# A new order of the same steps in a fused attention and token-mixing kernel

## The chip, the cores and the metric

The kernel runs on one core of one Trainium2 chip. The metric is the device time of one execution in microseconds (us); the kernel before took 115.36 us as the median of 13 runs, from 114.9 to 115.99. Five engines work side by side: PE (TensorE, matmuls and transposes), ACT (ScalarE), DVE (VectorE), POOL (GpSimd) and SP (SyncE). Each runs its own program in order, and they wait for one another and for DMA transfers through semaphores.

## The reference

There are eight batches of eight heads, 576 positions and a head size of 64. First, 32 packed queries `p` per head attend to `k` and `v`; the result is at once key and value of a second attention, with `q` as its queries. The heads are then laid side by side into `x` (576 x 512), which goes through a mixing of tokens with a ReLU and a last product.

```python
p_packed = sm_attn(p, k, v)
x = heads_side_by_side(sm_attn(q, p_packed, p_packed))
wq, wk = x @ w_q, x @ w_k
W_tok = scale * einsum('bsd,btd->bst', wq, wk)
out = maximum(einsum('bst,btd->bsd', W_tok, x), 0) @ w_out
```

## The kernel before

One batch is one round of the same chain of steps, and the rounds of neighbouring batches overlap. The name of a step is its kind, its batch and its part: `S1.3.2` is part 2 of step S1 of batch 3. In the order in which one batch needs them:

- KT transposes k (PE, L298; for batch 0 from float32), and KE copies the result out of PSUM. S1 multiplies it with the packed queries (PE, L322), X1 is the exponential on ACT (L328), and PV multiplies with v (PE, L340). RC and PP (L345, L349) divide and mask on DVE, PT transposes (L356), and PE (the step) copies.
- The packed queries of all batches are prepared once by PX (L257, L268) and PXE.
- QT transposes q (PE, L386), QE copies. S2 multiplies with the packed result (PE, L405), X2 is the exponential on ACT (L414), RS and RR sum and invert on DVE (L421, L425), and AM multiplies the two (L431) on POOL or on DVE. AT transposes that (PE, L440), AE copies.
- QK multiplies the packed result with the weights of the mixture (PE, L365), QKE copies; WC, once, copies a part of these weights on POOL (L133). WKQ forms both projections (PE, L456 and L461), WE and WR copy them, GM and Y reduce over tokens (PE, L478 and L488) with GE and YE as copies, MX and MR mix (PE, L504 and L509), and RL and RLR apply the ReLU.
- OT multiplies with w_out (PE, L536), OE copies to SBUF, and the stores go out on the queue of SP (the very last on that of ACT).

WARM steps (L603) are matmuls on zeros, without use for the output; there are ten of them, of 256 to 1024 columns in float32.

The loads are LD steps. `LD.K0` and `LD.K1` (the halves of k of batch 0), `LD.p0` and `LD.p1` go over the queues of ACT and SP. All others are issued by POOL: `P` (the packed queries of the other batches), `q`, `k` and `v` of a batch (576 KB each), `W` (four transfers for both weights of the mixture) and `O` (two transfers for w_out). k and q have four buffers each, so have the v tiles. POOL issues these loads in its own program, between its AM and WC steps; the wait of a load for its buffer or its place is thus a wait of POOL.

All of this is put into one sequence by the string ORDER (L10 on), written out in full. Every word is a step, with the PSUM bank after `=` and the engine after `@` (A for ACT, V for DVE, P for POOL). The loop at the end walks through it and emits the instructions in that order, so the order of the words is the order of each engine's program:

```python
for item in ORDER.split():
    name, _, bk = item.partition("=")
    name, _, eng = name.partition("@")
    f = name.split(".")
    if f[0] == "LD":
        d = load(f[1])
        if item == end:
            release(d)
```

`end` is the last LD of the string. Stores that come before it in the order are held, and start only when that load has landed; those after it go out as they come.

The softmax here doesn't subtract the row's maximum and nothing guards it: scores larger than these inputs give would overflow.

## Time and profile before

| | |
|---|---|
| median of 13 runs | 115.36 us |
| the profiled execution | 115.01 us |
| its span, first to last instruction | 113.0 us |
| granted TensorE clock | 0.997 |
| PE busy | 104.2 us |
| ACT, DVE, POOL busy | 82.9, 73.3, 38.3 us |
| DMA, mean | 225 GB/s |
| loads of POOL's queue, share of 16 engines | 73.6% |

The span is the time from the first to the last instruction of the profiled execution; 2.0 us lie around it. PE here is the busy time of matmuls; PEld, where it stands, is that of weight loads, which overlap matmuls. The idle time of an instruction's engine just before it stands in square brackets, with the event that ended it; that event is inferred from semaphores, and the last one is named where several were waited for. A landing is the time from the issue of a DMA to its last byte.

### The profile page before, as it was taken

Reading aid. Unit: us, or ns where it says so; the run is one execution under the profiler, and the core shown is the slowest. Engines: PE = TensorE matmul, PEld = TensorE weight load, DVE = VectorE, ACT = ScalarE, POOL = GpSimd, SP = SyncE. Lnnn points to the kernel's source line nnn. Section 1 sums busy time; section 2 is a strip of 40 time slices with the busy share of each in tenths; the row PEclk is TensorE's granted clock in tenths of the full one; section 3 lists DMA queues with packets and bytes.
Section 4 is the critical chain, followed back from the end, with each engine's and each line's share of the span. In section 5 each row is a group of like instructions: output and inputs, shape, how many; then the busy total and the mean of one; then the engine's idle time right before and its main releaser. Section 6 shows DMA issues by size and latency. Waiting matters only on the chain.

```text
span 113.0 us, 4280 instructions
## 1 busy us (share of the span) xinstructions
PE 104.2 (92%) x1842; PEld 73.5 (65%) x1855; DVE 73.3 (65%) x186; ACT 82.9 (73%) x169; POOL 38.3 (34%) x49
## 2 busy tenths in 40 slices
PE   4899979999999999999999999999999999999910
PEld 2167967588785867698858786794985664644500
DVE  2053767966897567797785898389688484916300
ACT  0008595998995896799988866997999989958420
POOL 6952226692290000558093094013008053000000
PEclk9999999999999999999999999999999999999998
DMA  1999999999999999999999999991899999993994
GB/s 50 377 219 204 208 192 208 211 203 208 206 210 211 209 213 207 215 203 208 210 208 208 217 206 201 202 191 35 286 295 321 304 355 315 321 319 100 299 315 133
DMA packets 16035, 25.44 MB, mean 225 GB/s; under 512 B 2656, under 2 KB 10848, under 8 KB 16016
## 3 DMA queue, kind: packets, MB, share of 16 engines
q0 software_dynamic: 11792, 14.42, 73.6%
q1 hardware_dynamic: 3872, 9.90, 26.5%
q10 hardware_dynamic: 352, 0.85, 2.2%
q8 instruction: 14, 0.23, 0.7%
q14 instruction: 5, 0.04, 0.1%
HBM read 30.15 MB, written 9.44 MB: 350 GB/s over the span
## 4 chain that ended last, share of the span: by engine, by line
PE 84%; ACT 6%; DMA 4%; issue 1%
PE out_ps L536 28%; PE kT_ps L298 8%; PE qT_ps L386 7%; PE pv_ps L340 6%; PE aT_ps L440 5%; DMA k_sb<-in_k_dram 4%; PE e_ps L322 4%; PE wkq_ps L461 4%; PE e_ps L405 4%; PE mix_ps L504 4%; PE warm_ps L603 4%; PE wkq_ps L456 2%; PE g_ps L478 2%; PE y_ps L488 2%; PE pqk_ps L365 1%; PE px_ps L268 1%
## 5 line engine op out<-in xcount | busy, mean ns | idle before, releaser
L431 POOL TENSOR_TENSOR a<-e,rr 128x512 bf16<-128x512 f32 (+1 forms) x13 | 16.1, 1245 | 45.8 <-DVE rr L425 22.2
L536 PE MATMUL out_ps<-wout,relu 128*128 128x512 bf16 (+1 forms) x120 | 30.6, 373 | 0.6
L131 ACT ACTIVATE o<-out_ps 128x512 f32<-128x512 f32 (+1 forms) x26 | 15.3, 590 | 7.6 <-PE out_ps L536 7.4
L536 PEld LDWEIGHTS <-relu 128*128 128x128 bf16 x132 | 11.7, 98 | 10.1 <-issue 0.3
L421 DVE TENSOR_REDUCE rs<-e 128x16 f32<-128x512 f32 (+1 forms) x16 | 12.9, 809 | 3.2 <-ACT e L414 3.0
L514 ACT ACTIVATE relu<-mix_ps 128x512 bf16<-128x512 f32 x21 | 11.5, 607 | 1.4 <-PE pv_ps L340 1.2
L603 PE MATMUL warm_ps<-warm 128*128 128x512 f32 (+1 forms) x24 | 10.8, 580 | 1.5 <-DVE warm L138 1.5
L414 ACT ACTIVATE e<-e_ps 128x512 f32<-128x512 f32 (+1 forms) x24 | 11.6, 529 | 0.7 <-PE e_ps L405 0.5
L131 ACT ACTIVATE qT<-qT_ps 128x1024 bf16<-128x1024 bf16 (+1 forms) x12 | 9.8, 831 | 2.4 <-PE qT_ps L386 2.4
L328 ACT ACTIVATE e<-e_ps 128x512 bf16<-128x512 f32 (+1 forms) x24 | 11.2, 501 | 0.2 <-PE e_ps L322 0.2
L386 PE MATMUL qT_ps<-idb,q_sb 128*64 128x128 bf16 x288 | 10.9, 220 | 0.0
L298 PE MATMUL kT_ps<-idb,k_sb 128*128 128x128 bf16 x126 | 9.9, 220 | 0.0
L386 PEld LDWEIGHTS <-q_sb 128*64 128x64 bf16 x288 | 8.8, 110 | 0.7 <-issue 0.3
L135 DVE COPY kT<-kT_ps 128x1024 bf16<-128x1024 bf16 (+1 forms) x14 | 7.8, 565 | 2.0 <-PE kT_ps L298 2.0
L516 DVE TENSOR_SCALAR relu<-mix_ps 128x512 bf16<-128x512 f32 x11 | 7.3, 686 | 2.6 <-PE mix_ps L504 2.0
L340 PE MATMUL pv_ps<-v_sb,e 64*64 64x192 bf16 x288 | 8.4, 244 | 0.6 <-ACT e L328 0.6
L298 PEld LDWEIGHTS <-k_sb 128*128 128x128 bf16 x126 | 7.5, 98 | 1.3 <-issue 0.4
L461 PE MATMUL wkq_ps<-aT,pqk 128*128 128x256 bf16 (+1 forms) x64 | 7.9, 233 | 0.0
L131 ACT ACT_TABLE_LOAD x1 | 1.3, 1283 | 8.7 <-DVE idb L210 8.7
L135 DVE COPY o<-out_ps 128x512 f32<-128x512 f32 (+1 forms) x7 | 4.6, 653 | 4.7 <-PE out_ps L536 3.7
L182 POOL DMA_DIRECT2D k_sb<-in_k_dram x7 | 5.3, 763 | 6.3 <-PE warm_ps L603 2.7
L322 PE MATMUL e_ps<-pdiag,kT 128*64 128x64 bf16 x288 | 7.4, 197 | 0.0
(81 smaller groups left out, 199.6 us busy)
## 6 DMA issues: line engine op xcount, KB each, us to landing
out_dram<-o SPq DMA_DIRECT2D x31, 256.0 KB, 3.9
q_sb<-in_q_dram POOLq DMA_DIRECT2D x8, 576.0 KB, 13.1
v_sb<-in_v_dram POOLq DMA_DIRECT2D x8, 576.0 KB, 11.7
k_sb<-in_k_dram POOLq DMA_DIRECT2D x7, 576.0 KB, 13.2
out_dram<-o_rem SPq DMA_DIRECT2D x4, 256.0 KB, 3.8
k_sb<-in_k_dram ACTq DMA_DIRECT2D x1, 576.0 KB, 4.9
k_sb<-in_k_dram SPq DMA_DIRECT2D x1, 576.0 KB, 7.5
wout<-in_moe_w_out_dram POOLq DMA_DIRECT2D x2, 256.0 KB, 12.5
```

What stands on the lines that cost most here:

```text
L131: nc.scalar.activation(o, i, COPY)
L135: nc.vector.tensor_copy(o, i)
L298: nc.tensor.transpose(ps[:, n], src[:, o:o + P], idb if b else idf)
L322: nc.tensor.matmul(ps[halves(i), at[0]:at[1] + 1:at[1] - at[0]], T["kT", b][:, place(b, m), halves(i)], rhs, start=True, stop=True)
L340: nc.tensor.matmul(T["pv", b][i][halves(cc)], lhsT, rhs, start=n == 0, stop=n == R - 1, skip_group_check=True)
L386: nc.tensor.transpose(o[halves(x)], q_in[b][:, x, r * Dh:(r + 1) * Dh], idb)
L414: nc.scalar.activation(e2(b, min(c, 1))[:, o:o + n], T["s2", b, c].rearrange("a t i c (x l) -> a (t i c x) l", l=L), EXP, scale=scale)
L421: e.tensor_reduce(rs, T["e2", (b, d)], axis=AX, op=ADD)
L431: e.tensor_tensor(a2[:, 2 * d:2 * d + n].rearrange("a t i (u l) -> a (t i u) l", l=L), T["e2", (b, d)], T["rr", (b, d)].to_broadcast((P, n ...
L461: nc.tensor.matmul(ps[:, e:e + c1 - c0], pqk[:, i, Dl:], aT[:, i, c0:c1], start=i == 0, stop=i == 1)
L536: nc.tensor.matmul(ps, lhsT, wout[:, j, x:x + w], start=j == 0, stop=j == NJ - 1)
L603: nc.tensor.matmul(ps[:, 0:n], warm[:, 0:P], warm[:, 0:n], start=True, stop=True)
```

## The change

The string ORDER is replaced by another. It has the same 664 steps, with the same shapes; their sequence differs nearly throughout, 90 of them are given to another engine for the copy or the elementwise operation, and most have another PSUM bank. Nothing else in the file changes. The order in which POOL issues its loads:

```
before: P q0 v0 k1 W q1 v1 k2 k3 O v2 q2 v3 q3 k4 q4 k5 v4 q5 k6 v5 q6 q7 k7 v6 v7
after:  P q0 v0 W k1 q1 v1 k2 k3 O v2 q2 v3 k4 q3 k5 v4 q4 k6 q5 v5 q6 v6 k7 v7 q7
```

The beginning and the end of both strings (the first 16 and the last few lines of each):

```diff
-LD.p0 LD.K0 LD.K1 LD.p1 LD.P SET.warm@V LD.q0 SET.aT1@V WARM.0=0 SET.idf@V LD.v0 SET.aff@P
-KT.0.0=1 KT.0.1=2 WARM.1=3 PX.0=4 LD.k1 KT.0.3=5 KT.0.4=6 KE.0.0@V KE.0.1@V LD.W SET.pd0@V
-PXE.0.1@A SET.idb@V PXE.0.0@A KE.0.4@V KE.0.3@V KT.0.2=7 PX.1=0 PX.2=1 LD.q1 QT.0.1=2 KE.0.2@A
-SET.v0@V S1.0.1=3 QE.0.1@A QT.0.0=4 S1.0.0=6 S1.0.2=5 PX.8=7 SET.mask@V X1.0.1@A X1.0.2@A X1.0.0@A
-PV.0.0=2,3 QT.0.2=5 SET.pd1@V LD.v1 QE.0.0@A LD.k2 PXE.8.1@V RC.0.1@V RC.0.0@V SET.v1@V WARM.5=6
-WARM.6=4 PXE.2.1@A SET.aT0@V LD.k3 WARM.9=6 PP.0.0@V PP.0.1@V QE.0.2@V PT.0=4 PE.0@A KT.1.2=2
-WARM.2=3 S2.0.0=5 KT.1.1=6 PXE.1.0@V LD.O S2.0.1=4 PXE.2.0@A S2.0.2=3 KT.1.0=1 SET.v2@V X2.0.0@A
-RS.0.0@V RR.0.0@V X2.0.2@A X2.0.1@A KE.1.0@A AM.0.0@P RS.0.1@V WARM.7=5 WC.0@P RR.0.1@V WARM.8=3
-WARM.4=5 PXE.8.0@A AT.0.0=4 KE.1.1@V KE.1.2@A S1.1.0=3 LD.v2 S1.1.2=1 QT.1.0=5 PXE.1.1@A AE.0.0@A
-QT.1.1=7 SET.wm@V SET.aT2@V AM.0.1@V X1.1.0@A QK.0=2 QKE.0@A S1.1.1=6 X1.1.1@A QT.1.2=0 AT.0.1=4
-WKQ.0.0=3 AT.0.2=2 X1.1.2@A PV.1.0=6,1 QE.1.0@V AE.0.1@A PV.1.1 AE.0.2@V PV.1.2 WE.0.0@A QE.1.1@A
-RC.1.0@V WKQ.0.2=5 WKQ.0.1=2 WARM.3=4 RC.1.1@V WE.0.1@A PP.1.0@V LD.q2 QE.1.2@A LD.v3 PP.1.1@V
-PT.1=3 WR.0@V GM.0=7 PE.1@V S2.1.0=6 GE.0@V S2.1.1=1 KT.2.2=4 Y.0=5 KT.2.0=2 LD.q3 KE.2.2@V
-S2.1.2=0 X2.1.0@A RS.1.0@V YE.0@A X2.1.1@A MX.0.0=3,7 MX.0.1=6,4 KE.2.0@V X2.1.2@A KT.2.1=5 LD.k4
-RL.0.0@A S1.2.0=1 RR.1.0@V QK.1=0 S1.2.2=2 KT.3.2=3 RL.0.3@A AM.1.0@P KT.3.1=4 RL.0.2@A RS.1.1@V
-QKE.1@A X1.2.2@A AT.1.0=7 KE.3.2@A KT.3.0=0 RL.0.1@A RR.1.1@V AM.1.1@V AT.1.2=2 AE.1.0@V AE.1.2@A
...
-RL.6.2@V RL.6.3@A RL.6.1@V WKQ.7.0=3 RL.6.0@A WE.7.0@A OE.5.4@V WKQ.7.1=1 WKQ.7.2=4 MR.6=0
-WE.7.1@V RLR.6@A OT.6.2=6 WR.7@V OE.6.2@A GM.7=5 GE.7@A OT.6.1=7 Y.7=2 OT.6.3=3 YE.7@V OE.6.1@A
-MX.7.0=1,0 MX.7.1=4,6 MR.7=5 RL.7.2@V OE.6.3@A RLR.7@A OT.6.0=7 RL.7.0@V OT.7.4=2 RL.7.1@A
-RL.7.3@A OT.7.2=3 OT.7.3=0 OE.6.0@V OE.7.4@A OT.7.1.1=5 OE.7.3@A OE.7.2@V OT.7.1.0=1 OE.7.1.0@A
-OT.7.0=4 OE.7.1.1@V OE.7.0@A
+LD.p0 LD.K0 LD.K1 LD.p1 SET.warm@V SET.aT1@V SET.mask@V SET.pd0@V LD.P LD.q0 WARM.1=0 LD.v0
+SET.idf@V SET.aff@P PX.0=1 KT.0.0=2 SET.v1@V LD.W WARM.0=3 SET.wm@V KT.0.3=4 KT.0.2=5 SET.idb@V
+SET.pd1@V KE.0.0@A KT.0.1=6 KT.0.4=7 WARM.3=0 PX.1=2 KE.0.1@A LD.k1 QT.0.2=3 QT.0.0=0 KE.0.3@A
+PXE.0.0@V KE.0.2@V PXE.0.1@A SET.aT0@V LD.q1 SET.v0@V KE.0.4@V S1.0.2=5 S1.0.0=6 LD.v1 X1.0.0@A
+QT.0.1=4 S1.0.1=7 X1.0.1@A X1.0.2@A QE.0.0@V QE.0.2@A WARM.9=1 PV.0.0=0,6 RC.0.0@V LD.k2 WARM.8=7
+PX.2=5 QE.0.1@A PP.0.0@V LD.k3 RC.0.1@V PXE.1.1@A LD.O PP.0.1@V PT.0=1 PX.8=3 PE.0@V SET.aT2@V
+PXE.2.0@A S2.0.0=4 S2.0.2=0 X2.0.0@A WARM.6=7 PXE.8.1@A S2.0.1=6 SET.v2@V WC.0@P WARM.7=1
+PXE.8.0@V KT.1.2=7 KT.1.0=4 RS.0.0@V LD.v2 KE.1.2@V X2.0.1@A X2.0.2@A RR.0.0@V RS.0.1@V LD.q2
+KT.1.1=3 S1.1.2=1 QK.0=6 LD.v3 WARM.2=7 KE.1.1@V RR.0.1@V AM.0.0@P AT.0.0=0 LD.k4 AM.0.1@V
+PXE.1.0@A KE.1.0@A S1.1.1=2 X1.1.2@A QT.1.1=7 S1.1.0=4 AE.0.0@V PXE.2.1@A QT.1.2=3 X1.1.1@A
+QKE.0@A LD.q3 AT.0.1=1 AT.0.2=5 QE.1.2@V X1.1.0@A AE.0.2@V WKQ.0.0=2 WKQ.0.2=0 WARM.4=6 WE.0.0@A
+AE.0.1@V WKQ.0.1=3 WR.0@V WE.0.1@V PV.1.0=5,4 PV.1.1 PV.1.2 RC.1.0@V RC.1.1@V QT.1.0=1 GM.0=6
+PP.1.0@V PP.1.1@V PT.1=2 WARM.5=0 QE.1.1@A QE.1.0@V GE.0@A PE.1@A Y.0=7 S2.1.2=3 S2.1.0=5 X2.1.0@A
+KT.2.2=4 S2.1.1=6 YE.0@V X2.1.1@A MR.0=1 KT.2.0=0 KE.2.2@V RS.1.0@V S1.2.2=2 X2.1.2@A QK.1=7
+MX.0.1=4,5 RR.1.0@V RLR.0@A X1.2.2@A QKE.1@A MX.0.0=6,3 AM.1.0@P RS.1.1@V RL.0.0@A KT.2.1=1
+KT.3.2=2 KE.2.0@A RR.1.1@V AM.1.1@P KE.3.2@V KE.2.1@V KT.3.0=7 KT.3.1=6 AT.1.0=2 AE.1.0@V S1.2.1=1
...
+AT.7.0=2 OE.5.0@A AM.7.1@V RLR.4@V QKE.7@A AT.7.2=7 YE.6@V MR.5=0 AT.7.1=6 AE.7.1@A AE.7.2@V
+MX.6.1=4,1 AE.7.0@A RLR.5@V MX.6.0=3,5 RL.6.1@V RL.6.0@A OT.5.4=7 RL.6.3@V WKQ.7.2=0 WKQ.7.1=6
+OE.5.4@V RL.6.2@A WE.7.1@A WKQ.7.0=4 WR.7@V WE.7.0@A OT.6.3=2 GM.7=3 OT.6.2=1 MR.6=5 OE.6.3@A
+GE.7@A Y.7=7 OT.6.1=0 YE.7@V RLR.6@V MX.7.0=6,4 MX.7.1=2,3 MR.7=7 RL.7.0@V OE.6.2@A OT.6.0=1
+OE.6.1@A RL.7.3@A RLR.7@V OT.7.4=5 RL.7.2@V RL.7.1@A OT.7.2=0 OE.6.0@A OT.7.3=6 OT.7.1.1=3
+OT.7.1.0=7 OE.7.1.1@V OE.7.4@A OT.7.0=2 OE.7.2@A OE.7.3@A OE.7.1.0@V OE.7.0@A
```

In POOL's program the first AM step, `AM.0.0@P`, and the copy `WC.0@P` stand after the loads of O and before v2 in the order before; in the order after, WC stands there, and AM.0.0 stands after v3.

## The prediction

> **What bounds the kernel now.** I read the shares of busy time first, then what PE waited for, then PE, POOL and the landings in order of time. PE carries the page:

> ```profile
> PE 104.2 (92%) x1842; PEld 73.5 (65%) x1855; DVE 73.3 (65%) x186; ACT 82.9 (73%) x169; POOL 38.3 (34%) x49
> ```

> The waits of PE (line waited for: us in all, times, longest) are three, all before 15 us:

> ```profile
> PE warm_ps L603 <- DVE warm L138: 1.5, 1, 1.5
> PE pv_ps L340 <- ACT e L328: 0.6, 1, 0.6
> PE kT_ps L298 <- DMA k_sb<-in_k_dram: 0.5, 1, 0.5
> ```

> Busy time by stretches (PE first, then PEld, DVE, ACT, POOL) says that from 22.1 us to the last matmul at 107.7 PE is full:

> ```profile
> 0.00:22.10 22.10, 19.42 (x239) 13.07 (x239) 11.65 (x34) 10.71 (x18) 11.18 (x21) 1.00 1.07 208
> 22.10:76.80 54.70, 54.24 (x1196) 41.88 (x1204) 41.63 (x105) 46.57 (x100) 21.69 (x25) 1.00 1.17 207
> 76.80:107.70 30.90, 30.54 (x410) 18.54 (x414) 19.97 (x49) 25.02 (x53) 5.46 (x5) 1.00 0.82 271
> ```

> So the end is the moment at which PE's dense run starts, plus a fixed amount of matmul work, plus any bubble that a new order puts into it, plus 5.3 us of last eviction and store. The dense run starts with AT.0.0 (aT_ps, L440), which transposes the output of AM.0.0 on POOL (a, L431). PE in order of time (start, us) around it:

> ```profile
> 20.05 1.94 PE L603 MATMUL warm_ps<-warm 128*128 128x256 f32 x6
> 22.13 0.40 PE L440 MATMUL aT_ps<-idb,a 128*128 128x128 bf16 x4
> ```

> And POOL, which issues the loads and runs AM.0.0 in one program:

> ```profile
> 9.14 0.71 POOL L186 DMA_DIRECT2D q_sb<-in_q_dram  x1 [2.07 <-DMA pbf<-in_p_dram]
> 12.05 0.76 POOL L178 DMA_DIRECT2D v_sb<-in_v_dram  x1 [2.20 <-DMA q_sb<-in_q_dram]
> 14.65 0.74 POOL L182 DMA_DIRECT2D k_sb<-in_k_dram  x1 [1.84 <-DMA v_sb<-in_v_dram]
> 18.06 0.74 POOL L182 DMA_DIRECT2D k_sb<-in_k_dram  x1 [2.67 <-PE warm_ps L603]
> 18.79 1.24 POOL L174 DMA_DIRECT2D wout<-in_moe_w_out_dram  x2
> 21.03 1.05 POOL L431 TENSOR_TENSOR a<-e,rr 128x512 bf16<-128x512 f32 x1 [1.00 <-DVE rr L425]
> 22.03 0.39 POOL L133 COPY wqk<-wqk 128x256 bf16<-128x256 bf16 x1
> 22.37 0.81 POOL L178 DMA_DIRECT2D v_sb<-in_v_dram  x1
> 23.17 0.72 POOL L186 DMA_DIRECT2D q_sb<-in_q_dram  x1
> 23.87 0.79 POOL L178 DMA_DIRECT2D v_sb<-in_v_dram  x1
> ```

> Count POOL's DMAs: P, q0, v0, k1, four of W, then q1 is the ninth, and it waits until the first (P) has landed; v1, the tenth, waits for the second (q0); k2 for the third. Issue plus time to landing: P 1.27+7.6 = 8.9, q1 issued 9.14; q0 1.98+9.8 = 11.8, v1 issued 12.05; k1 3.83+13.7 = 17.5, k3 (twelfth, four after eight) issued 18.06; k2 (eleventh) 14.65+11.9 = 26.5, k4 (nineteenth) issued 27.11. The names on the last two idle times are other engines, but the landings fit. So each DMA of POOL waits for the landing of the one eight places earlier, and is issued 0.25 to 0.55 us after it.

> [...] POOL idles 2.07 us before q1. [...] POOL here runs in program order throughout. [...]

> **The change, part by part.** *Work.* The 664 steps are the same set, so PE's work is the same: 275 PE steps, with equal sums. Ninety steps change engine. Priced by the rows of each form (AE 0.611 on ACT, 0.415 on DVE; RLR 0.466, 0.423; WE 0.502, 0.552; YE 0.386, 0.425; QKE 0.506, 0.550; AM of 128x768 1.480 on POOL, 0.940 on DVE), ACT loses 3.3 us, DVE gains 3.3, POOL loses 1.9. They stay near 71%, 68% and 32%, so I cost this at nothing: PE hides it. Without that cover DVE's 3.3 us would be the price.

> *Front, up to AT.0.0 on PE.* The first warm matmuls end at 5.24 as now. Then PX.0, KT.0.0 and WARM.0 (about 0.8, 0.6 and 1.8) fill until 8.5; K1 lands at 1.19+7.5 = 8.7; four groups KT.0.* (0.5, 0.5, 0.5, 0.2), WARM.3 (0.5) and PX.1 (0.5) reach 11.4; q0 lands at 11.8; QT.0, S1.0 and WARM.9 (0.14+0.5+0.06+0.27+0.5+0.27+0.86) reach 14.6; v0 is there at 2.74+11.6 = 14.3. PV.0 (0.9) ends at 15.5, against 15.84 now. Then, up to AT.0.0: WARM.8 0.86, PX.2 0.75, PT.0 0.13, PX.8 0.74, S2.0.0 and S2.0.2 0.5, WARM.6 0.5, S2.0.1 0.25, WARM.7 0.5, KT.1 1.0, S1.1.2 0.16, QK.0 0.27, WARM.2 0.5: 6.2, so PE is at AT.0.0 at 21.7. Set on its own chain, AM.0.0 could start at 20.5: X2.0.0 ends at 18.8, RS.0.0 0.69, then KE.1.2 (0.28, after KT.1.2 at 19.9) stands before RR.0.0 (0.25). It would be done by 21.6 and PE would not wait.

> *POOL.* But AM.0.0 is moved. Now it stands right behind the two loads of O. In the new program POOL has q1, v1, k2, k3, O, O, WC.0, v2, q2, v3, and only then AM.0.0. v2 (0.81) and q2 (0.72) have free places (W has long landed; q2 waits for k1, at about 18.2, W now being ahead of it). v3 is the seventeenth DMA and waits for the ninth, q1. The bytes ahead of q1 are the same set in both orders and the DMA engines are full (share 1.07), so it lands as now:

> ```profile
> q_sb<-in_q_dram POOLq DMA_DIRECT2D x1, 576.0 KB, 11.8
> ```

> that is 9.14+11.8 = 20.9. v3 is issued 0.25 to 0.55 later and takes 0.79: 22.0 to 22.3. AM.0.0 takes 1.05: 23.05 to 23.35. AT.0.0 follows 0.05 later, as now, at 23.1 to 23.4, after a PE stall of about 1.5 us; behind it in PE's order stand S1.1.1, QT.1.1 and all the rest.

> *Sum.* AT.0.0 moves from 22.13 to 23.1..23.4: +1.0 to +1.3. The steps of PE left from there are longer by QK.0's, S1.1.2's and WARM.3's absence against WARM.4 and WARM.5: sums 82.74 against 82.48, times 1.04 for changes of operation: +0.27. Together +1.25 to +1.55; I take +1.35, the earlier issue being what three of the five waits show. The next chain is covered: QKE.0 on ACT, behind S1.1.1 and X1.1.1, ends at about 24.7, and WKQ.0.0, which needs it, is reached at 25.2.

> *Later loads.* k4 moves ahead of q3, k5 and v4 ahead of q4, k6 of q5, v6 of k7, q7 to the end. Landings come every 2.85 us or so and the places are shared out anew. By PE's summed steps the new order needs q2 at about 39.8 (lands 37.7), k5 at 51.5 (49.6), q4 at 56.6 (54.8); the others have more. Now the smallest margins are k7's (lands 59.55+13.2 = 72.75, used at 72.77) and q4's (49.6, used at 50.31). So nothing is lost, and nothing large was there to win. The other AMs behind loads (AM.1.0 behind q3, which waits for k2 at 26.5 and is out by 27.8; AM.2.1 behind k6, 34.9; AM.3.0 behind q5, 37.7) are wanted 3 us and more later. The last load ends at about 77 as now, so the held stores start as now. The last seven OT stand in the same order and the last eviction is on ACT again (0.60): nothing.

> The profiled execution took 115.01 us, 113.0 of span and 2.0 around it. Its sum is 113.0+1.35+2.0 = 116.4. The median of the runs, 115.36, is 0.35 above that execution, so the forecast is 116.7.

> **Rivals.** (1) *Not slower: POOL isn't held.* If v3 gets its place before about 19.7, AM.0.0 starts at 20.5 and AT.0.0 is reached at 21.7 to 21.8: -0.35, plus 0.27, about -0.1, hence 115.3. It decides if q1 lands by 19.5 rather than 20.9, or if v3's wait is for an older DMA. For it: v3 in the trace of before was issued long after q1 landed, so its own wait isn't seen. Against: five other loads show the rule of eight. If ACT's front also runs shorter than my 0.9 us a copy, and the earlier PP.0 (two memsets, 0.54 and 0.12, no longer stand before it) is worth its 0.7 us, it would be 114.6.
> (2) *More bubbles.* Short covers in the new order are GM.2 to Y.2 (0.35 us of PE work for an eviction of 0.28 and its hand-over), AT.0.2 to WKQ.0.2 (0.37 for 0.22), PV.1 to PT.1 (1.0 for two RC and two PP, 0.98). Each could cost 0.1 to 0.3, and DVE's 3.3 us more could add others: 117.2 to 118. Against: before has covers as short (GM.0 to S2, AT.0.2) and no wait.
> (3) *The clock falls.* [...]

> **How the numbers follow.** Held as computed, 116.2 to 117.3: 0.58. Held with more bubbles or a clock drop, 117.3 to 119: 0.17. Held for less, 115.7 to 116.2: 0.06. Not held, within 0.3% (about what a measurement of this kernel can tell from no change, 0.35 us): 0.10. Not held and faster: 0.09. Slower is the sum of the first three, 0.81. The range leaves out one tenth at each end: 115.3 to 118.0.

> **What would show it.** Right: POOL issues v3 at about 21.3 and AM.0.0 starts at about 22.1; PE waits 1 to 2 us for POOL's a (L431) at L440; AT.0.0 at about 23.1; no other PE wait over 0.5 us; last matmul at about 109. Wrong: AM.0.0 before 21; or waits at L461, L488 or L405 that sum to over 1 us; or a PE wait for k_sb, q_sb or v_sb after 25 us.

## The result, and the profile after

The kernel after takes 117.29 us (median of 11 runs, 116.17 to 117.91), the kernel before beside it 115.56 us (48 runs). The ratio is 1.0135, with a 95% interval of 1.0106 to 1.0163: slower. The medians lie 1.73 us apart, and 1.35% of 115.56 is 1.56 us; 1.35 us was forecast, and 117.29 lies inside the range of 115.3 to 118.0.

The median hides what the single times show. They fall into two groups with a gap between them: 116.17, 116.29, 116.37, 116.5, 116.57, and 117.29, 117.32, 117.38, 117.6, 117.67, 117.91. The middle of the lower group is 116.37, that of the upper one 117.49; the forecast of 116.7 lies in between. The ratios in this text leave out runs more than 1.5% above the fastest of their kernel as disturbed; where a kernel has two groups of times of its own, as here, all times count and both groups are told.

The profiled execution (117.67 us, span 115.6) is of the upper group. Its busy times:

```profile
PE 106.6 (92%) x1841; PEld 73.7 (64%) x1855; DVE 76.1 (66%) x196; ACT 81.4 (70%) x160; POOL 36.5 (32%) x48
```

PE is busy 2.4 us longer with the same work. Its waits (line waited for: us in all, times, longest):

```profile
PE warm_ps L603 <- DVE warm L138: 1.5, 1, 1.5
PE wkq_ps L456 <- DVE aT L135: 0.3, 1, 0.3
PE qT_ps L386 <- issue: 0.2, 1, 0.2
PE aT_ps L440 <- ACT kT L131: 0.2, 1, 0.2
PE out_ps L536 <- ACT aT L131: 0.2, 1, 0.2
```

The wait that was forecast, 1 to 2 us at L440 for POOL's `a`, isn't there: PE waits 0.2 us at that line, and the wait is put down to ACT's copy of kT. That name can't be right, because this copy ends at 23.55 and AT.0.0 starts at 23.54. AM.0.0 ends at 23.48, and in all thirteen traces of this text AT.0.0 starts 0.06 us after AM.0.0's end, whatever name stands beside the wait. So PE does wait for `a`, but it only gets there at 23.38, and what is left to wait for is 0.16 us. AT.0.0 starts 0.14 us behind the forecast's 23.1 to 23.4. POOL in order of time (start, us):

```profile
8.45 0.71 POOL L186 DMA_DIRECT2D q_sb<-in_q_dram  x1 [1.37 <-DMA pbf<-in_p_dram]
...
16.79 0.78 POOL L178 DMA_DIRECT2D v_sb<-in_v_dram  x1
17.60 0.71 POOL L186 DMA_DIRECT2D q_sb<-in_q_dram  x1
20.97 0.76 POOL L178 DMA_DIRECT2D v_sb<-in_v_dram  x1 [2.67 <-DMA q_sb<-in_q_dram]
22.43 1.05 POOL L431 TENSOR_TENSOR a<-e,rr 128x512 bf16<-128x512 f32 x1 [0.71 <-DMA v_sb<-in_v_dram]
```

POOL does what the prediction says up to v3: q1 is issued at 8.45 and lands 12.2 us later, at 20.65; POOL idles 2.67 us ahead of v3 and issues it at 20.97, 0.32 after that landing. But AM.0.0 (L431) doesn't start when v3 is out, at 21.73. It waits 0.71 us more. The name in the brackets is a load; what was late is on DVE, which has just inverted the sums that AM.0.0 multiplies with:

```profile
22.05 0.23 DVE L425 RECIPROCAL rr<-rs 128x16 f32<-128x16 f32 x1
```

RR.0.0 ends at 22.28 and AM.0.0 starts at 22.43. So in this execution the chain PE, ACT, DVE that feeds AM.0.0 was itself late, by more than POOL. Where it lost its time is seen at the start of PE. First the kernel before:

```profile
1.46 3.78 PE L603 MATMUL warm_ps<-warm 128*128 128x512 f32 x4 [1.46 <-DVE warm L138]
5.77 1.42 PE L298 MATMUL kT_ps<-idf,k_sb 128*128 128x128 f32 x8 [0.53 <-DMA k_sb<-in_k_dram]
7.03 1.88 PE L603 MATMUL warm_ps<-warm 128*128 128x512 f32 x4
8.84 0.74 PE L257 MATMUL px_ps<-idf,p 32*128 32x32 f32 x9
```

and then the kernel after:

```profile
1.46 3.78 PE L603 MATMUL warm_ps<-warm 128*128 128x512 f32 x4 [1.46 <-DVE warm L138]
5.17 1.16 PE L257 MATMUL px_ps<-idf,p 32*128 32x32 f32 x9
6.26 1.11 PE L298 MATMUL kT_ps<-idf,k_sb 128*128 128x128 f32 x4
7.17 3.57 PE L603 MATMUL warm_ps<-warm 128*128 128x512 f32 x4
...
22.68 0.70 PE L603 MATMUL warm_ps<-warm 128*128 128x256 f32 x2
23.54 0.40 PE L440 MATMUL aT_ps<-idb,a 128*128 128x128 bf16 x4 [0.16 <-ACT kT L131]
```

The second block of warm matmuls (WARM.1 before, WARM.0 after) is the same work: 1.88 us before, 3.57 us after. The first block, on a PE that has just begun, takes 3.78 us in both. A record of this block takes 1.06 us at the slow pace (the median of the eight records after) and 0.59 at the other (the shortest before), so PE ran its second block at about half speed too (3.57 us against 1.88). In the traces' own record of the granted clock, whose values are 0.5 and 1, it goes to full at 6.51 us before, and at 10.56 after; the row PEclk of the page shows 9 in its first slices in both, so only durations and that record tell it. PE reaches AT.0.0 at 23.4 and not at 21.7, and everything that feeds AM.0.0 is late with it.

From there on, by stretches (PE, PEld, DVE, ACT, POOL, then clock, DMA share and GB/s):

```profile
0.00:22.10 22.10, 20.64 (x235) 13.22 (x235) 10.09 (x36) 10.13 (x17) 12.67 (x23) 1.00 1.07 210
22.10:76.80 54.70, 53.45 (x1146) 40.30 (x1152) 42.33 (x107) 45.90 (x93) 20.13 (x22) 1.00 1.16 203
76.80:110.00 33.20, 32.46 (x471) 20.20 (x471) 23.66 (x55) 25.19 (x52) 3.74 (x4) 1.00 0.81 263
```

PE is as full as before. From the start of AT.0.0 to the end of the last OT are 85.52 us before (22.13 to 107.66) and 86.04 after (23.54 to 109.58). The profiled spans differ by 2.6 us: 1.41 by a later AT.0.0, 0.52 in the dense run, 0.70 in the tail behind it (5.36 against 6.06). The dense run and the tail vary from execution to execution: a second execution of the same kernel has 85.59 and 5.55, and the tail is 5.36 to 6.57 in the five traces of orders built on before and 5.55 to 6.32 in the eight built on after. So only the front can be put down to the change. The profile names two causes there: POOL's hold of AM.0.0, as forecast, and a clock that comes up late. In this execution the clock is the one that counts. With the hold alone, AM.0.0 would have started behind v3 at 21.73 and AT.0.0 at about 22.84 (an estimate from the lines above), 0.7 us earlier than it did.

### The profile page after: what moved, and what is told of

It reads as the page before. It is cut to its first block, busy times and chain, and to the rows that moved or that the text cites. A ratio compares the mean times of both kernels' runs of the same rounds, so it can differ in the third digit from the quotient of the medians.

```text
span 115.6 us, 4278 instructions
## 1 busy us (share of the span) xinstructions
PE 106.6 (92%) x1841; PEld 73.7 (64%) x1855; DVE 76.1 (66%) x196; ACT 81.4 (70%) x160; POOL 36.5 (32%) x48
## 4 chain that ended last, share of the span: by engine, by line
PE 87%; ACT 5%; issue 1%; DVE 1%
PE out_ps L536 27%; PE warm_ps L603 9%; PE qT_ps L386 7%; PE kT_ps L298 7%; PE pv_ps L340 6%; PE e_ps L322 5%; PE aT_ps L440 4%; PE e_ps L405 4%; PE wkq_ps L461 4%; PE mix_ps L504 3%; PE wkq_ps L456 2%; PE g_ps L478 2%; PE px_ps L257 2%; PE y_ps L488 1%; ACT relu L514 1%
## 5 line engine op out<-in xcount | busy, mean ns | idle before, releaser
L431 POOL TENSOR_TENSOR a<-e,rr 128x512 bf16<-128x512 f32 (+1 forms) x12 | 14.3, 1190 | 47.8 <-DVE rr L425 18.1
L131 ACT ACTIVATE o<-out_ps 128x512 f32<-128x512 f32 x27 | 16.2, 599 | 8.9 <-PE out_ps L536 7.5
L603 PE MATMUL warm_ps<-warm 128*128 128x512 f32 (+1 forms) x24 | 13.6, 672 | 1.5 <-DVE warm L138 1.5
L414 ACT ACTIVATE e<-e_ps 128x512 f32<-128x512 f32 (+1 forms) x24 | 11.6, 527 | 3.1 <-PE e_ps L405 2.8
L131 ACT ACTIVATE kT<-kT_ps 128x1024 bf16<-128x1024 bf16 (+2 forms) x8 | 6.4, 808 | 9.0 <-PE kT_ps L298 9.0
L328 ACT ACTIVATE e<-e_ps 128x512 bf16<-128x512 f32 (+1 forms) x24 | 11.5, 508 | 1.6 <-PE e_ps L322 1.5
L514 ACT ACTIVATE relu<-mix_ps 128x512 bf16<-128x512 f32 x20 | 10.9, 614 | 0.9 <-PE mix_ps L504 0.7
L298 PE MATMUL kT_ps<-idb,k_sb 128*128 128x128 bf16 x126 | 9.4, 219 | 0.0
L131 ACT ACTIVATE qT<-qT_ps 128x1024 bf16<-128x1024 bf16 (+1 forms) x12 | 9.0, 783 | 0.0
L135 DVE COPY qT<-qT_ps 128x1024 bf16<-128x1024 bf16 (+1 forms) x12 | 6.9, 576 | 2.6 <-PE qT_ps L386 2.6
L516 DVE TENSOR_SCALAR relu<-mix_ps 128x512 bf16<-128x512 f32 x12 | 8.1, 683 | 0.7 <-PE mix_ps L504 0.5
L340 PE MATMUL pv_ps<-v_sb,e 64*64 64x192 bf16 x288 | 8.4, 245 | 0.0
L298 PEld LDWEIGHTS <-k_sb 128*128 128x128 bf16 x126 | 7.6, 98 | 0.8 <-issue 0.2
L440 PE MATMUL aT_ps<-idb,a 128*128 128x128 bf16 x80 | 7.6, 220 | 0.2 <-ACT kT L131 0.2
L461 PE MATMUL wkq_ps<-aT,pqk 128*128 128x256 bf16 (+1 forms) x64 | 7.8, 233 | 0.0
L178 POOL DMA_DIRECT2D v_sb<-in_v_dram x8 | 6.2, 773 | 4.5 <-DMA q_sb<-in_q_dram 4.5
## 6 DMA issues: line engine op xcount, KB each, us to landing
q_sb<-in_q_dram POOLq DMA_DIRECT2D x8, 576.0 KB, 12.0
v_sb<-in_v_dram POOLq DMA_DIRECT2D x8, 576.0 KB, 11.6
k_sb<-in_k_dram POOLq DMA_DIRECT2D x7, 576.0 KB, 13.9
k_sb<-in_k_dram ACTq DMA_DIRECT2D x1, 576.0 KB, 4.4
k_sb<-in_k_dram SPq DMA_DIRECT2D x1, 576.0 KB, 6.8
```

The lines of the kernel that those rows point to most:

```text
L131: nc.scalar.activation(o, i, COPY)
L135: nc.vector.tensor_copy(o, i)
L298: nc.tensor.transpose(ps[:, n], src[:, o:o + P], idb if b else idf)
L340: nc.tensor.matmul(T["pv", b][i][halves(cc)], lhsT, rhs, start=n == 0, stop=n == R - 1, skip_group_check=True)
L431: e.tensor_tensor(a2[:, 2 * d:2 * d + n].rearrange("a t i (u l) -> a (t i u) l", l=L), T["e2", (b, d)], T["rr", (b, d)].to_broadcast((P, n ...
L440: nc.tensor.transpose(ps[:, i, t - 2 * c], T["a2", b][:, t, i], idb)
```

## The experiments

Two theories. *Hold*: AM.0.0 stands behind v3, which waits for q1's landing. *Clock*: what stands between the first two blocks of warm matmuls keeps PE at half clock for longer, in part of the executions. Each has an edit that removes it alone. All orders below compute the same output; the WARM steps, which some of them move or leave out, are no part of it. The kernel before had medians of 115.31, 115.27 and 115.18 us beside the experiments (x1 to x4, x5 to x8, x9 to x11).

**x1: after, without the hold.**

```diff
-KT.1.1=3 S1.1.2=1 QK.0=6 LD.v3 WARM.2=7 KE.1.1@V RR.0.1@V AM.0.0@P AT.0.0=0
+KT.1.1=3 S1.1.2=1 QK.0=6 AM.0.0@P LD.v3 WARM.2=7 KE.1.1@V RR.0.1@V AT.0.0=0
```

> The changed kernel with one word moved: AM.0.0@P stands before LD.v3 again, behind LD.q2. Two theories. Hold (the prediction's): the dense run of PE starts late because AM.0.0 waits on POOL behind v3, which waits for the landing of q1. Then this gives the 1.35 us back: 117.3 - 1.35 = 115.9, AM.0.0 at about 20.5. Clock (new, from the trace of the changed kernel): PE itself reaches AT.0.0 only at 23.4 because WARM.0 ran at half clock (3.57 us in place of 1.8), and the 11 times fall into two groups, 116.2 to 116.6 and 117.3 to 117.9. Then the upper group stays at 117.3 to 117.9 in this kernel and its median stays within 0.4 of 117.3. Both, in turns (hold in runs with the clock up early, PE in the others): lower group 115.6, upper group unchanged.

Measured: median 117.01 (13 runs), in two groups again: 113.96, 114.94, 115.09, 115.17, and nine from 116.28 to 117.93 (middle 117.31). The profiled execution is of the upper one. PE, then POOL:

```profile
7.17 3.62 PE L603 MATMUL warm_ps<-warm 128*128 128x512 f32 x4
```

```profile
18.11 0.74 POOL L186 DMA_DIRECT2D q_sb<-in_q_dram  x1
22.64 1.04 POOL L431 TENSOR_TENSOR a<-e,rr 128x512 bf16<-128x512 f32 x1 [3.79 <-DVE rr L425]
23.64 0.81 POOL L178 DMA_DIRECT2D v_sb<-in_v_dram  x1
```

POOL is free from 18.85 and waits 3.79 us for RR.0.0. The hold is gone and AM.0.0 is as late as before the edit. Between the lower groups the edit gains 1.1 us (116.37 to 115.0, less the 0.25 by which the kernel before was lower beside x1 to x4 than beside after); between the upper ones, nothing (117.49 to 117.31, less the same 0.25). So the hold is real and isn't alone.

**x2: after, with the two blocks of warm matmuls side by side**, the hold left in.

```diff
-LD.P LD.q0 WARM.1=0 LD.v0 SET.idf@V SET.aff@P PX.0=1 KT.0.0=2 SET.v1@V LD.W WARM.0=3
+LD.P LD.q0 WARM.1=0 WARM.0=3 LD.v0 SET.idf@V SET.aff@P PX.0=1 KT.0.0=2 SET.v1@V LD.W
```

> The changed kernel with WARM.0 moved directly behind WARM.1, ahead of PX.0 and KT.0.0: 2048 columns of warm matmuls in one piece, so that the clock is up by the end of them in every run. Hold: no change, 117.3, because AM.0.0 still ends at 22.9 to 23.4. Clock: the upper group disappears, -1.5 to -1.9 against it, all times at 115.5 to 115.9. Both: the upper group disappears and all times stand at the lower group's 116.2 to 116.6, with AT.0.0 at about 22.9 behind AM.0.0.

Measured: 116.6 us (6 runs; five of them from 116.44 to 116.72, and one at 117.63, which was not profiled and stays unexplained), ratio 1.0122 (1.0085 to 1.0159). Here is the trace that the prediction described. PE's waits, PE and POOL:

```profile
PE warm_ps L603 <- DVE warm L138: 1.5, 1, 1.5
PE aT_ps L440 <- POOL a L431: 1.2, 1, 1.2
```

```profile
1.46 5.97 PE L603 MATMUL warm_ps<-warm 128*128 128x512 f32 x8 [1.46 <-DVE warm L138]
...
20.79 0.70 PE L603 MATMUL warm_ps<-warm 128*128 128x256 f32 x2
22.70 0.40 PE L440 MATMUL aT_ps<-idb,a 128*128 128x128 bf16 x4 [1.21 <-POOL a L431]
```

```profile
20.81 0.76 POOL L178 DMA_DIRECT2D v_sb<-in_v_dram  x1 [2.06 <-DMA q_sb<-in_q_dram]
21.59 1.06 POOL L431 TENSOR_TENSOR a<-e,rr 128x512 bf16<-128x512 f32 x1
```

All eight records of warm matmuls take 5.97 us together, where after they took 7.35 (3.78 and 3.57). PE reaches AT.0.0 at 21.5, and now it stands 1.21 us for AM.0.0, which follows v3 with no gap. The clock's delay is gone, and the hold's cost is in view.

**x3: both edits together.**

> Both edits together: AM.0.0@P ahead of LD.v3, and WARM.0 directly behind WARM.1. Hold: as the first, 115.9. Clock: as the second, 115.5 to 115.9. Both: 115.3 to 115.7, below either edit alone, in one group. Third possibility, that the rest of the new order has bubbles of its own: over 116.2 although AT.0.0 stands at 22.0 or earlier.

Measured: 115.31 us (22 runs, 114.13 to 116.15), ratio 0.9981 (0.9959 to 1.0004): no difference from before that can be told.

```profile
21.14 1.04 POOL L431 TENSOR_TENSOR a<-e,rr 128x512 bf16<-128x512 f32 x1 [1.97 <-DVE rr L425]
```

So the two causes make up the whole loss. With the warm blocks side by side, the hold costs 116.6 - 115.31 = 1.3 us. The other steps of the change (90 moved engines, the later loads, other banks) are worth nothing together that can be told: the dense run is 85.61 us here, 85.52 before.

**x4: the hold alone, put into the kernel before.** LD.v2, LD.q2 and LD.v3 go in front of AM.0.0, which stands where it stood.

```diff
-X2.0.1@A KE.1.0@A AM.0.0@P RS.0.1@V
+X2.0.1@A KE.1.0@A LD.v2 LD.q2 LD.v3 AM.0.0@P RS.0.1@V
```

> The kernel before with LD.v2, LD.q2 and LD.v3 moved ahead of AM.0.0@P (nothing else): the hold by itself. Hold: POOL issues O until 20.0, then v2, q2, v3 until 22.3 (q1 has landed at 20.9), AM.0.0 from 22.3 to 23.35 in place of 21.03 to 22.08, AT.0.0 1.27 later: 115.5 + 1.25 = 116.8. Clock: the beginning of PE's order is unchanged, so 115.5, if AM.0.0's delay finds slack.

Measured: 115.95 us (19 runs), 0.64 above before by the medians and 0.36 by the ratio, 1.0031 (1.0009 to 1.0053). Slower, but by half or less of the 1.25 us that was expected.

```profile
17.59 0.74 POOL L182 DMA_DIRECT2D k_sb<-in_k_dram  x1 [3.11 <-PE ppT_ps L356]
18.32 1.24 POOL L174 DMA_DIRECT2D wout<-in_moe_w_out_dram  x2
19.54 0.78 POOL L178 DMA_DIRECT2D v_sb<-in_v_dram  x1
20.28 0.74 POOL L186 DMA_DIRECT2D q_sb<-in_q_dram  x1
20.98 0.80 POOL L178 DMA_DIRECT2D v_sb<-in_v_dram  x1
21.75 1.10 POOL L431 TENSOR_TENSOR a<-e,rr 128x512 bf16<-128x512 f32 x1
```

The miss teaches something. None of these instructions waits after k3: v3 found q1 landed already (8.40 + 12.2 = 20.6), and what delays AM.0.0 is the time that POOL needs to issue the five DMAs between k3 and it, 3.4 us from 18.32. It starts 0.72 us later than before (21.75 against 21.03), AT.0.0 0.78 later (22.91 against 22.13), and the median moves by 0.64. The price of a step behind loads is thus the later of two things, the landing that the last load waits for and POOL's own issue time. In the order after it is the landing (an idle time of 2.06 to 2.67 us stands before v3), in this one the issues.

**x5: the clock alone, put into the kernel before.** PX.0 goes between the first two blocks of warm matmuls, and KT.0.1 behind them, as in the order after.

```diff
-SET.aff@P KT.0.0=1 KT.0.1=2 WARM.1=3 PX.0=4 LD.k1
+SET.aff@P PX.0=4 KT.0.0=1 WARM.1=3 KT.0.1=2 LD.k1
```

> The kernel before with PE's beginning of the changed kernel: WARM.0, PX.0, KT.0.0, WARM.1, KT.0.1 in place of WARM.0, KT.0.0, KT.0.1, WARM.1, PX.0; POOL's order, the loads and all else unchanged. Clock: [...] WARM.1 then takes 3.6 us in place of 1.9 and all behind it is 1.2 to 1.9 later: an upper group at 116.5 to 117.2 beside times at 115.3, median over 115.7. Hold and load order: no change, 115.3.

Measured: median 116.28 (23 runs), in two groups, nine times from 115.01 to 115.51 (middle 115.23) and fourteen from 116.0 to 118.23 (middle 116.97). The gap between them is only 0.5 us, and before itself reached 116.12 beside it, so the lowest two or three of the fourteen may belong to the lower group. The profiled execution is of the upper group:

```profile
5.17 1.17 PE L257 MATMUL px_ps<-idf,p 32*128 32x32 f32 x9
6.26 1.12 PE L298 MATMUL kT_ps<-idf,k_sb 128*128 128x128 f32 x4
7.17 3.23 PE L603 MATMUL warm_ps<-warm 128*128 128x512 f32 x4
```

Two steps moved within PE's program, with no POOL instruction touched, split the times of the kernel before: the lower group stays at 115.2, the upper one is 1.7 us above it. That is the clock's cost with no hold to hide in. As in after, only an execution of the upper group was profiled; that the lower one has an early clock is inferred.

**x9: which of the two neighbours matters?** In x2 the two blocks are side by side; in after, PX.0 and KT.0.0 stand between them. x9 is x1 with PX.0 alone moved behind the second block, and KT.0.0 left between.

```diff
-SET.aff@P PX.0=1 KT.0.0=2 SET.v1@V LD.W WARM.0=3 SET.wm@V
+SET.aff@P KT.0.0=2 SET.v1@V LD.W WARM.0=3 PX.0=1 SET.wm@V
```

> The changed kernel with AM.0.0@P ahead of LD.v3 and with PX.0 moved behind WARM.0, so that KT.0.0 alone (four 128-row transposes) stands between the two warm matmuls, as KT.0.0 and KT.0.1 do in the kernel before. It tells whether the nine 32-row transposes of PX.0 keep the clock down or the mere separation of the warm matmuls. PX.0 is the cause: no upper group beyond the spread of the repaired kernel, 114.1 to 116.2, median 115.3. Separation is the cause: two groups as with AM.0.0 moved alone, 114.0 to 115.2 and 116.3 to 117.9, median about 117.

Measured: 115.37 us (22 runs, 114.33 to 116.13, one group), ratio 0.9992 (0.9968 to 1.0015).

```profile
5.55 1.02 PE L298 MATMUL kT_ps<-idf,k_sb 128*128 128x128 f32 x4 [0.31 <-DMA k_sb<-in_k_dram]
6.41 1.88 PE L603 MATMUL warm_ps<-warm 128*128 128x512 f32 x4
8.22 0.74 PE L257 MATMUL px_ps<-idf,p 32*128 32x32 f32 x9
```

The block takes 1.88 us although KT.0.0 and even an idle time of 0.31 us stand in front of it. It is PX.0, nine transposes of 32 rows, and not a pause between the blocks or transposes as such. Against x1, which differs in this one word, the upper group of 117.31 is gone: 1.9 us.

The clock records show where PX.0 acts. In all thirteen traces any two changes of the clock lie a whole multiple of 3.413 us apart (the 105.81 us between the two changes of before are 31 times that, the 102.40 of after 30 times). In these traces, then, the clock changes at ticks of this spacing, and the executions begin at different places between two ticks: the clock is full from 5.41 us in x7, from 6.51 in before, from 7.57 in x3. In the trace of before the clock rose at 6.51. In x5's trace it rose at 9.88, so the tick before that was at 6.47, nearly the same place, and there it stayed at half. In the 3.41 us up to that tick, before has 2.14 us of warm matmuls, 0.74 of 128-row transposes and 0.53 of idle time; x5 has 2.18, 0.14, no idle time, and 1.09 of PX.0. A longer pause is no rival either: in x10 the clock rose at 7.38 after 1.27 us of warm matmuls, 1.70 of 128-row transposes and 0.45 of idle time.

```profile
5.69 1.88 PE L298 MATMUL kT_ps<-idf,k_sb 128*128 128x128 f32 x8 [0.45 <-DMA k_sb<-in_k_dram]
```

**x11: the kernel after once more**, a single execution, for a second profile.

> The changed kernel as it is, for a second profile, since its first one fell into the upper of its two groups. If it falls into the lower (116.1 to 116.6): clock up by 6.5, WARM.0 in 1.9, AM.0.0 at about 21.7 right behind v3, PE waiting 1 to 1.5 us for it at L440, AT.0.0 at 22.7 to 22.9. If into the upper: as the first, AT.0.0 at 23.5, AM.0.0 behind rr.

Measured: 116.94 us, with the clock late again (second block 3.62 us; full clock at 11.01). The time lies between after's two groups, but the kernel before was 0.38 us lower beside it than beside after, which puts it with the upper one.

```profile
20.95 0.76 POOL L178 DMA_DIRECT2D v_sb<-in_v_dram  x1 [2.10 <-DMA q_sb<-in_q_dram]
22.66 1.05 POOL L431 TENSOR_TENSOR a<-e,rr 128x512 bf16<-128x512 f32 x1 [0.95 <-DMA v_sb<-in_v_dram]
```

v3 is held until 20.95 here too, and AM.0.0 starts at 22.66, as in x1, which has no hold (22.64). With a late clock the hold ends too early to matter. No execution of the lower group of after has been profiled; x2 stands in for it.

**x6: before, with the order of loads of after** in the same places of the string, all engines else as before.

```diff
-P q0 v0 k1 W q1 v1 k2 k3 O v2 q2 v3 q3 k4 q4 k5 v4 q5 k6 v5 q6 q7 k7 v6 v7
+P q0 v0 W k1 q1 v1 k2 k3 O v2 q2 v3 k4 q3 k5 v4 q4 k6 q5 v5 q6 v6 k7 v7 q7
```

> The kernel before with the changed kernel's sequence of loads, put into the same places of the order (W ahead of k1, k4 ahead of q3, k5 and v4 ahead of q4, k6 of q5, v6 of k7, q7 last). If the order of loads costs by itself: W's small packets ahead of k1 and the wait of K T.1 for it move the beginning by 0.5 or more, 115.8 and above, and a load that comes too late shows as a PE wait for q_sb or v_sb (q3 and q4 land 2.8 us later here and their places in PE's order have 1 to 2 us): +1 to +3, 116.3 to 118. Clock and hold: nothing from the beginning, 115.3 with at most the waits just named.

Measured: 121.83 us (6 runs), ratio 1.0466 (1.039 to 1.0542). PE's waits, and PE in order of time:

```profile
PE qT_ps L386 <- DMA q_sb<-in_q_dram: 3.8, 2, 2.7
...
PE kT_ps L298 <- DMA k_sb<-in_k_dram: 0.6, 2, 0.5
```

```profile
54.59 0.43 PE L386 MATMUL qT_ps<-idb,q_sb 128*64 128x128 bf16 x4 [2.70 <-DMA q_sb<-in_q_dram]
...
55.58 0.62 PE L461 MATMUL wkq_ps<-aT,pqk 128*128 128x256 bf16 x2
```

The prediction costs the later loads at nothing, because PE's order was changed along with them. That holds: after has no PE wait for a load behind its front. The run shows that it holds only for both together: the same loads under the old order of PE cost 6.6 us (121.83 against 115.27). In the profiled execution, 120.52 us, the dense run is 91.05 us against before's 85.52. Of these 5.5 us, 3.8 are the two waits for q. About 1.5 (an estimate, half of PE's work in that stretch) come with a clock that is at half from 54.08 to 57.49, of which PE works 2.9 us; it shows in the second line, where two matmuls take 0.62 us that take 0.38 at full clock (before, at 24.82). Of the 0.6 us for k, 0.5 stand at the front, as in before.

**x7, x8, x10: are the warm matmuls still needed?** With x3's edits PE isn't held by POOL any more, and fills its time ahead of AT.0.0 with WARM steps. x7 is x3 without WARM.8; x8 leaves out WARM.6, WARM.7 and WARM.2 as well; x10 is before without WARM.9.

```diff
-QE.0.2@A WARM.9=1 PV.0.0=0,6 RC.0.0@V LD.k2 WARM.8=7 PX.2=5
+QE.0.2@A WARM.9=1 PV.0.0=0,6 RC.0.0@V LD.k2 PX.2=5
```

> The changed kernel with both repairs (AM.0.0@P ahead of LD.v3, WARM.0 behind WARM.1) and without WARM.8, 512 columns of filler (1.13 us) between PV.0 and PX.2. If PE's own work up to AT.0.0 sets the start of the dense run: PT.0 waits for PP.0 instead, at 16.7 in place of 17.25, all 0.6 earlier: 114.7. If ACT's chain (PXE.2.0, X2.0, PXE.1.0, KE.1.0, PXE.2.1) sets it: 115.0 to 115.3.

> As the one before, and WARM.6, WARM.7 and WARM.2 (256 columns each, 0.5 us each) left out too; like WARM.8 they are no part of the output. PE's work up to AT.0.0: 1.5 us less again, but the chain S2.0.0, X2.0.0, RS, RR, AM.0.0 (3.4 us from S2.0.0 to AT.0.0) stands behind it, so AT.0.0 at most 0.3 to 0.6 earlier than without WARM.8 alone: 114.2 to 114.7. If ACT sets it, the same as without WARM.8; if the clock falls in the gaps, 116 and above.

> The kernel before without WARM.9 (512 columns of filler between PV.0 and PT.0, no part of the output). If the start of the dense run sets the end in this order too: PT.0, at 17.83 now, follows PP.0's end at 17.3 instead, 0.5 earlier, 114.8. If ACT's chain up to AT.0.0 (ppT, PXE.1.0, X2.0, KE.1.0 to 22.1) sets it: 115.1 to 115.3.

Measured: x7 114.72 us (22 runs, 114.05 to 115.72), ratio 0.9954 (0.9931 to 0.9978); x8 114.76, ratio 0.995 (0.9929 to 0.9972); x10 115.25, ratio 0.9995 (0.9971 to 1.0019). x7's POOL and PE:

```profile
19.69 1.04 POOL L431 TENSOR_TENSOR a<-e,rr 128x512 bf16<-128x512 f32 x1 [0.89 <-DVE rr L425]
```

```profile
20.80 0.40 PE L440 MATMUL aT_ps<-idb,a 128*128 128x128 bf16 x4 [0.15 <-ACT kT L131]
```

In the order after, one warm step of 0.86 us sat on the path that sets AT.0.0: without it the median is 0.59 us below x3's, and the kernel beats both before and after. The traces show more than that, AM.0.0 at 19.69 in place of x3's 21.14, but the two executions differ in the clock too: it was up at 5.41 in x7 and at 7.57 in x3, and 2.16 us at half clock are worth about 1.1 (an estimate, half of them). Leaving out three more steps gains nothing. In x8 PE waits 0.8 us at L440, again under the name of ACT's kT; AT.0.0 starts at 21.54, 0.06 after AM.0.0's end, and AM.0.0 had waited 1.22 us for RR.0.0. So the chain over ACT and DVE that feeds AM.0.0 has become the later one. In the kernel before a warm step of the same size is covered; there x10 finds nothing to gain, and before's other warm steps were not tried. With AM.0.0 and the warm blocks moved and WARM.8 left out, the new order is thus half a per cent faster than the old one.

## Why the prediction was right and wrong

**Right: the bound.** The time is set by the start of AT.0.0 plus a fixed dense run. The dense run is between 85.2 and 86.0 us in every profile but x6's, whose loads come too late. Nothing else of the change moves the time: the engine moves show as +2.8 us on DVE, -1.5 on ACT and -1.8 on POOL (3.3, 3.3 and 1.9 by the prediction's sum), with one new bubble of 0.3 us at WKQ.0.0. The view names DVE's aT, but AE.0.0 had ended at 25.22, and WKQ.0.0 starts at 25.84, 0.05 after QKE.0 ends on ACT. That is the chain which the prediction called covered, by 24.7 against 25.2; it isn't, by 0.3 us. This is all there is of rival (2).

**Right: POOL's hold, its place and its size.** v3 waits for q1's landing; both profiles of after and that of x2 show it issued 0.24 to 0.33 us after (20.97 against 20.65, 20.95 against 20.71, 20.81 against 20.48). The prediction has v3 at 21.2 to 21.5 and AM.0.0 at 22.0 to 22.3; x2, with the clock up, has 20.81 and 21.59, 0.4 earlier since q1 landed earlier. The PE stall came out at 1.21 against 1.5, the price at 1.3 against 1.35. The price rests on the medians: in its one trace x2 has AT.0.0 at 22.70, only 0.57 after before's and not 1.0 to 1.3, and 0.75 of the 1.40 us between the two spans are tail. Rival (1), no hold, needed q1 to land by 19.5; it landed at 20.65. It stays a rule inferred from landings, now with three more of them.

**Wrong: the step "*Front, up to AT.0.0 on PE*".** It lets WARM.0 take 1.8 us, as WARM.1 does in the trace of before, and so has PE at AT.0.0 at 21.7. In both profiled executions of after it takes 3.6 us, PE is there at 23.4 and 23.6, and by their times six of the eleven were like that. A duration was carried over to a place where the engine ran at another speed. The sign by which the prediction wanted to be known, a PE wait of 1 to 2 us for `a`, is therefore missing in both profiles of after, although the hold is there; "AT.0.0 at about 23.1" came out at 23.54, but in those executions it was due to the late chain.

**The two costs don't add up, they overlap.** Both end in AM.0.0. Without the clock's delay, the hold costs 1.3 us (x2 against x3). Without the hold, the clock's costs 1.9 (x1's upper group against x9). With the hold in place, the clock's adds only 117.49 - 116.37 = 1.1; with a late clock, the hold adds 0.2 or less. This is why the forecast, with one of the two, lay near the truth: the other was partly hidden behind it. That is luck in part, since 116.7 lies between the two groups, 116.37 and 117.49, and in neither.

**Rival (3)** has the clock fall after the stall, an estimate of the author's that the trace of before doesn't show. It doesn't: stalls of 1.21 us (x2) and 1.57 us (x4) cost nothing beyond themselves, and the mean granted clock is 0.989 in both, against 0.973 in x6, where the clock did fall. The clock was the right suspect in the wrong place: it rose late at the start.

**The remainder.** "+0.27" for the leftover PE steps isn't seen in x3 (+0.09 in the dense run); it is within what the dense run varies. The lower group of after lies 0.8 us above before's median, not 1.3 as x2; and x1's lower group lies 0.3 below x3. So with the clock up, PX.0 in its early place may be worth some tenths. But a lower group holds only the executions with an early clock and x3's times hold all, which can lower it as well. No execution of a lower group was profiled, so this is left open.

## What to carry to other kernels

A duration belongs to a clock: when a step is moved within the first microseconds of PE's program, price it at both clocks (here 1.88 and 3.57 us for the same block), and look at single run times for groups before a median is explained. An elementwise step behind loads on the engine that issues them starts, as here, when the last of them is out: what it waited for was a landing in x2 (2.06 us idle before v3) and the time to issue five loads in x4 (3.4 us). Two delays that end in the same instruction hide each other (here 1.3 and 1.9 us alone, and only 1.1 for the second on top of the first), so remove both before saying what either is worth. After a reorder, try each filler again: one that was covered may now stand on the path. Before you believe the name beside a wait, compare the wait's end with the end of what is named.
